# One slot later: scores, outputs and splits in a kernel that interleaves a chunked scan with an MLP

## The chip, the cores and the metric

The kernel runs on one core of a Trainium2 chip. The metric is device time in microseconds: the median of three runs of the kernel before is 1139.93 us (1139.13 to 1140.27). Below, PE is the matrix engine (TensorE), DVE is VectorE, ACT is ScalarE, POOL is GpSimd and SP is SyncE, which here only issues DMAs.

## The reference, cut to what matters

A gated linear recurrence over 768 steps (4 batches, 8 heads of 48), then two gated MLPs (384 to 1536 to 384), the second behind an RMS norm:

```python
for t in range(S):
    state = alpha[:, :, t, :, None] * state + np.einsum('bhd,bhe->bhde', k[:, :, t], v[:, :, t])
    y[:, :, t] = np.einsum('bhd,bhde->bhe', q[:, :, t], state)
...
silu = g * (1.0 / (1.0 + np.exp(-g)))      # g = x @ w_gate
return (silu * val @ w_out)                # val = x @ w_val; second layer: x / rms * rms_g first
```

## The kernel before

The scan is cut into 24 chunks of 128 steps, numbered n = 0 to 23. A chunk is worked in slots T = 0 to 19, and a new chunk starts every 12 slots, so slots T = 12 to 19 of chunk n are the slots T = 0 to 7 of chunk n+1. `chunk(n, T)` (line 468) issues what a slot holds; in a slot the older chunk issues first. All engines run their instructions in the order in which they were issued.

In a chunk, DVE builds products of decays and merges them into q and k at seven levels (T = 0 to 6, `products` and `merge`; the merge at level 64 comes at T = 10), and ACT copies the merged halves (`copy_qk`). PE then makes the scores (`scores`, line 297, T = 8). DVE multiplies the scores of the low levels by masks (`masks`, line 318, T = 9 and 10) and ACT copies those of the two highest (`copies_p`, lines 326 and 329, T = 10). PE transposes k (line 477, T = 11), ACT copies the result to kt (line 529, T = 12), PE makes the outputs in three parts and the update of the state (`own_terms`, `outputs`, `kv`, lines 335 to 380, T = 14 and 16). ACT then copies the chunk's output to xhi, rounded (line 409, T = 17), DVE updates the state (lines 390 and 391, T = 17) and subtracts to get the remainder xlo (line 411, T = 18). Both xhi and xlo feed the MLP. Scores, k transposed and outputs of a chunk all lie in one accumulator tile Y of three banks, one after the other. Between parts of the outputs stands a tiny ACT read of Y ("order", line 485).

The tokens pass the first MLP in seven blocks of 3, 3, 3, 3, 4, 4 and 4 chunks. While PE works on one block, the slots of the next block's chunks are laid between its pieces. A block has 12 hidden steps f of three pieces: piece 0 is the gate product g, piece 1 the value product v, piece 2 the output product o of the hidden step before (nine matmuls each). Slots are issued behind the pieces: one slot behind each piece where the next block has three chunks (block 0, which does its own weight conversion, and blocks 1 and 2), and four slots a hidden step where it has four: one behind g, one behind v and two behind s*v and the o product (blocks 3 to 5). At a block's last piece the last chunk of the next block is at T = 19, so xhi and xlo of that chunk are made just ahead of the next block's first g. DVE multiplies silu(g), made by ACT, with v (line 655, "s"), ACT rounds it to hh (661) and DVE makes its remainder hl (667); o reads hh and hl one hidden step later. A finished block's o banks are copied out by ACT (`evac`, line 606) through two buffers `ev` and stored by SP.

Chunks 0 to 2 ("early", `n < BLOCKS[0][0]`) run ahead of the first block in banks of their own. Input loads stand in SP's queue in slots 15 to 19: q and k of chunk n+2, v of chunk n+1 by levels.

Of the kernel before, what the change touches and what calls it, by code (L numbers as in the profile page):

```python
# [19 lines left out]
B, H, S, D = 4, 8, 768, 48  # L20
# [3 lines left out]
NCH = B * NCB  # L24
# [31 lines left out]
class Kernel:  # L56
# [411 lines left out]
    def chunk(self, n, T):  # L468

        nc = self.nc  # L470
        more = n + B < NCH
        nxt = n + 1 if n + 1 < NCH else None

        if T == 11 and more:
            self.kp = (self.bank(n, "o2") if self.early(n) else self.Y[:, 2]).rearrange("s (p d) -> s p d", p=NP)
            for p in range(NP):
                nc.tensor.transpose(out=self.kp[:, p], in_=self.qk[n % 2][:, 1, p], identity=self.ident)  # L477
        if T == 14:
            self.own_terms(n)
            self.outputs(n, 0)  # L480
            if more:
                self.kv(n)
            self.outputs(n, 1)
        if T == 15 and not self.early(n):
            nc.scalar.activation(out=self.order, in_=self.Y[:, :, 0:1], func=AF.Copy)
        if T == 16:
            self.outputs(n, 2)
        early = self.early(n)
        if T == 6 and early:
            self.scores(n, range(4))  # L490
        if T == (9 if early else 8):
            self.scores(n, range(4 if early else 0, NL))

        if T == (15 if n < B else 17) and n + 2 < NCH:
            self.load_qk(n + 2)
        if T == 17 and nxt:
            self.load_vn(nxt)
        if nxt:
            for l in {17: (0, 1, 2), 18: (3, 4), 19: (5, 6)}.get(T, ()):
                if LEVELS[l] >= CDS[nxt]:  # L500
                    self.load_vl(nxt, l)

        if T == 17:
            self.split_x(n, 0)
            if more:
                self.state(n)
        if T == 18:
            self.split_x(n, 1)
        if T == 0:
            self.start_chunk(n)  # L510
            self.products(n, 1)
        if 1 <= T <= 6:
            self.merge(n, LEVELS[T - 1])
            self.products(n, LEVELS[T])
        if T == (7 if early else 9):
            self.masks(n, range(3))
        if T == 8 and early:
            self.masks(n, [3])
        if T == 10:
            self.masks(n, [4] if early else [3, 4])  # L520
            self.copies_p(n)
            self.merge(n, 64)
        if T == 11 and n >= B:
            for h in range(2):
                o = slice(64 * h, 64 * h + 64)
                nc.scalar.activation(out=self.Sd[o, :, 16 * h:16 * h + 16], in_=self.Sc[n % B][o, :, 32 - 32 * h:D - 32 * h], func=AF.Copy)
        if T == 12 and more:
            kt = self.kt[n] = self.a1.tile([128, NP, 128], F32, tag="kt", name="kt")
            nc.scalar.activation(out=kt, in_=self.kp, func=AF.Copy)
        if T == 1:  # L530
            self.direct = self.direct_ops(n)
        if 1 <= T <= 9:
            k = (1, 2, 2, 1, 2, 2, 2, 2, 9)[T - 1] if CDS[n] > 1 else T > 6
            for _ in range(min(k, len(self.direct))):
                self.direct.pop(0)()
            if T == 9 and nxt:
                for part in range(4):
                    self.load_dir(nxt, part)
# [319 lines left out]
```

## Time and profile before

| | |
|---|---|
| median of three runs | 1139.93 us |
| profiled execution, its own time | 1140.99 us |
| its span | 1139.2 us |
| PE busy | 1073.0 us, 94% |
| DVE busy | 654.4 us, 57% |
| ACT busy | 415.5 us, 36% |

The profiled execution is 1.06 us above the median. Block 0 starts at 69.93 us, block 1 at 172.89, block 2 at 246.64 (these and block 3 with 384 columns), block 4 at 406.36 and block 5 at 508.75 (with 512). A busy PE is full here, so its time is read from the gaps: the view of waits gives, for each engine, who ended its idle time. In a row of the timeline the first number is the start in us from the span's start, the second the time in us from the start of the first to the end of the last instruction of the row, and the bracket is the idle time ahead of it with what ended it. Matmuls overlap, so the next one is issued before the modelled end of the last.

### The profile page before, as it was taken

Reading aid. Unit: us, or ns where it says so; the run is one execution under the profiler, and the core shown is the slowest. Engines: PE = TensorE matmul, PEld = TensorE weight load, DVE = VectorE, ACT = ScalarE, POOL = GpSimd, SP = SyncE. Lnnn points to the kernel's source line nnn. Section 1 sums busy time; section 2 is a strip of 40 time slices with the busy share of each in tenths; the row PEclk is TensorE's granted clock in tenths of the full one; section 3 lists DMA queues with packets and bytes.
Section 4 is the critical chain, followed back from the end, with each engine's and each line's share of the span. In section 5 each row is a group of like instructions: output and inputs, shape, how many; then the busy total and the mean of one; then the engine's idle time right before and its main releaser. Section 6 shows DMA issues by size and latency. Waiting matters only on the chain.

```text
span 1139.2 us, 25598 instructions
## 1 busy us (share of the span) xinstructions
PE 1073.0 (94%) x10944; PEld 890.1 (78%) x10944; DVE 654.4 (57%) x1361; ACT 415.5 (36%) x770; POOL 46.0 (4%) x81
## 2 busy tenths in 40 slices
PE   2668999999999999999999999999999999999997
PEld 2645568999988877777888888888888888888886
DVE  4778867877777776766755877723322323233221
ACT  3456633443343433333334444422231222222212
POOL 2002000000000000000000000000000000000000
PEclk9779999999999999999999999999999999999999
DMA  8656534344354444335415333110000000100000
GB/s 255 178 176 224 158 78 113 96 125 117 103 131 124 124 123 116 109 92 141 118 39 182 123 132 132 42 56 1 28 28 1 28 28 1 56 1 1 28 1 28
DMA packets 56018, 103.64 MB, mean 91 GB/s; under 512 B 7392, under 2 KB 40672, under 8 KB 55904
## 3 DMA queue, kind: packets, MB, share of 16 engines
q1 hardware_dynamic: 50592, 80.37, 24.8%
q0 software_dynamic: 5312, 21.63, 5.7%
q8 instruction: 86, 1.41, 0.5%
q14 instruction: 28, 0.23, 0.1%
HBM read 89.00 MB, written 12.98 MB: 90 GB/s over the span
## 4 chain that ended last, share of the span: by engine, by line
PE 82%; DVE 3%; ACT 2%; DMA 2%; issue 1%; POOL 0%; SPq 0%; ACTq 0%; DVEq 0%
PE v L645 25%; PE g L645 25%; PE o L686 23%; PE Y L340 4%; PE Y L297 3%; DMA x2d<-ev 1%; ACT pt L326 1%; DVE pt L318 1%; PE Y L380 1%; DVE s L655 1%; PE Y L477 1%; ACT ev L606 1%; PE Y L335 1%; PE Y L584 0%; DVE x L167 0%
## 5 line engine op out<-in xcount | busy, mean ns | idle before, releaser
L655 DVE TENSOR_TENSOR s<-s,v 128x512 f32<-128x512 f32 (+1 forms) x156 | 100.7, 646 | 344.5 <-PE v L645 343.3
L645 PE MATMUL v<-xhi,w 128*128 128x512 f32 (+1 forms) x864 | 283.5, 382 | 0.0
L645 PE MATMUL g<-xhi,w 128*128 128x512 f32 (+1 forms) x864 | 282.1, 380 | 0.0
L686 PE MATMUL o<-hh,w 128*128 128x512 f32 (+1 forms) x864 | 208.4, 376 | 0.0
L661 ACT ACTIVATE hh<-s 128x512 fp32r<-128x512 f32 (+1 forms) x144 | 87.2, 606 | 295.3 <-DVE s L655 295.1
L645 PEld LDWEIGHTS v<-xhi,w 128*128 128x128 f32 x864 | 161.2, 188 | 28.1
L645 PEld LDWEIGHTS g<-xhi,w 128*128 128x128 f32 x864 | 161.2, 188 | 27.5
L686 PEld LDWEIGHTS o<-hh,w 128*128 128x128 f32 x864 | 159.7, 188 | 25.7
L652 ACT ACTIVATE s<-g 128x512 f32<-128x512 f32 (+1 forms) x156 | 87.6, 562 | 230.6 <-PE g L645 217.2
L645 PE MATMUL v<-xlo,w 128*128 128x512 f32 (+1 forms) x432 | 162.6, 376 | 0.0
L645 PE MATMUL g<-xlo,w 128*128 128x512 f32 (+1 forms) x432 | 162.6, 376 | 0.0
L686 PE MATMUL o<-hl,w 128*128 128x512 f32 (+1 forms) x432 | 117.9, 379 | 3.8 <-ACT ev L606 3.5
L667 DVE TENSOR_TENSOR hl<-s,hh 128x512 fp32r<-128x512 f32 (+1 forms) x144 | 94.4, 655 | 41.1 <-ACT hh L661 36.8
L686 PEld LDWEIGHTS o<-hl,w 128*128 128x128 f32 x432 | 79.6, 188 | 18.5 <-ACT ev L606 5.4
L645 PEld LDWEIGHTS g<-xlo,w 128*128 128x128 f32 x432 | 81.2, 188 | 12.9
L645 PEld LDWEIGHTS v<-xlo,w 128*128 128x128 f32 x432 | 81.2, 188 | 12.2
L230 DVE TENSOR_TENSOR qk<-qk,bpb 128x512 f32<-128x512 f32 x96 | 65.7, 685 | 9.3 <-ACT kc L253 7.0
L253 ACT ACTIVATE kc<-qk 128x512 f32<-128x512 f32 x72 | 45.3, 629 | 41.2 <-DVE qk L230 40.5
L340 PE MATMUL Y<-pt,vl 64*32 64x64 f32 (+1 forms) x2880 | 48.5, 229 | 4.3 <-issue 3.8
L340 PEld LDWEIGHTS Y<-pt,vl 64*32 64x32 f32 (+1 forms) x2880 | 41.5, 111 | 11.7 <-issue 7.5
L318 DVE TENSOR_TENSOR pt<-Y,mask 128x256 f32<-128x256 f32 x63 | 24.6, 419 | 22.7 <-PE Y L297 22.7
L230 DVE TENSOR_TENSOR qk<-qk,bpa 128x512 f32<-128x512 f32 x48 | 33.0, 687 | 4.7 <-ACT px L253 2.5
(117 smaller groups left out, 1031.1 us busy)
## 6 DMA issues: line engine op xcount, KB each, us to landing
vl<-vl SPq DMA_DIRECT2D x120, 128.0 KB, 3.9
qk<-qka SPq DMA_DIRECT2D x48, 288.0 KB, 4.7
room<-w POOLq DMA_DIRECT2D x36, 384.0 KB, 5.2
dir<-dirx SPq DMA_DIRECT2D x54, 192.0 KB, 3.2
wraw<-w SPq DMA_DIRECT2D x18, 384.0 KB, 3.8
room<-w SPq DMA_DIRECT2D x18, 384.0 KB, 4.1
vn<-vn SPq DMA_DIRECT2D x24, 192.0 KB, 4.7
x2in<-x2d SPq DMA_DIRECT2D x6, 768.0 KB, 4.3
```

The lines of the kernel that those rows point to most:

```text
L230: self.nc.vector.tensor_tensor(out=v, in0=v, in1=sub(t, o, [(1, 2), (2, nb), (0, b)]), op=ALU.mult)
L253: self.nc.scalar.activation(out=sub(t, 0, [(NP * 64, 2), (b, NP * 64 // b), (1, b)]), in_=v, func=AF.Copy)
L297: self.nc.tensor.matmul(out=sc[o:o + w, p] if l < 3 else sc[o:o + w, p // 2, p % 2], lhsT=kc[d, p, gs], rhs=qc[d, p, gs], start=True, stop ...
L318: self.nc.vector.tensor_tensor(out=p, in0=sc, in1=m, op=ALU.mult)
L326: nc.scalar.activation(out=split(self.pt32)[o:o + 32, :, :, g], in_=sc[o:o + 32, :, :, g], func=AF.Copy)
L340: mm = lambda o, a, x: self.nc.tensor.matmul(out=o, lhsT=a, rhs=x, start=False, stop=False, skip_group_check=True)
L645: nc.tensor.matmul(out=ps[:, :N], lhsT=a, rhs=x, start=(q == 0), stop=(q == len(ops) - 1))
L652: nc.scalar.activation(out=s[:, :N], in_=g[:, :N], func=AF.Silu)
L655: nc.vector.tensor_tensor(out=s[:, :N], in0=s[:, :N], in1=v[:, :N], op=ALU.mult)
L661: nc.scalar.activation(out=hh[:, :N], in_=s[:, :N], func=AF.Copy)
L667: nc.vector.tensor_tensor(out=hl[:, :N], in0=s[:, :N], in1=hh[:, :N], op=ALU.subtract)
L686: nc.tensor.matmul(out=O[gj][i][:, :N], lhsT=a[:, 128 * i:128 * i + 128], rhs=x[:, :N], start=(f == 0 and q == 0), stop=(f == NF - 1 and q ...
```

## The change

For chunks 3 to 23 these move: scores T = 8 to 9; masks of levels 1 to 4 from T = 9 to 10 (behind the copies and the merge at 64, which stay at T = 10), of level 8 inside T = 10 to the same place, of level 16 from T = 10 to 11; transposes of k T = 11 to 12; copy to kt 12 to 13; outputs and state product 14 to 15, the order read 15 to 16, third part of the outputs 16 to 17; xhi and state 17 to 18; xlo 18 to 19; loads of q and k for chunk n+2 from 17 to 18 (for chunk 3 from 15 to 18). Nothing is added or taken away.

```diff
-        if T == 11 and more:
+        early = self.early(n)
+        late = 0 if early else 1
+        if T == 11 + late and more:
...
-        if T == 14:
+        if T == 14 + late:
             self.own_terms(n)
             self.outputs(n, 0)
...
-        if T == 15 and not self.early(n):
+        if T == 15 + late and not early:
...
-        if T == 16:
+        if T == 16 + late:
             self.outputs(n, 2)
...
-        if T == (9 if early else 8):
+        if T == 9:
             self.scores(n, range(4 if early else 0, NL))
-        if T == (15 if n < B else 17) and n + 2 < NCH:
+        if T == (15 if early else 18) and n + 2 < NCH:
             self.load_qk(n + 2)
...
-        if T == 17:
+        if T == 17 + late:
             self.split_x(n, 0)
             if more:
                 self.state(n)
-        if T == 18:
+        if T == 18 + late:
             self.split_x(n, 1)
...
-        if T == (7 if early else 9):
+        if T == 7 and early:
             self.masks(n, range(3))
...
         if T == 10:
-            self.masks(n, [4] if early else [3, 4])
             self.copies_p(n)
             self.merge(n, 64)
+            if not early:
+                self.masks(n, range(4))
+        if T == 11 and not early:
+            self.masks(n, [4])
...
-        if T == 12 and more:
+        if T == 12 + late and more:
             kt = self.kt[n] = self.a1.tile([128, NP, 128], F32, tag="kt", name="kt")
```

What this does to the order on the engines is shown at three places, all around the start of block 4 (512 columns; the change shifts line numbers by a few). First PE, the transposes of chunk 16 ("ident,qk_88"), which stand between o of the block before and the second g. Before:

```order
L686 MATMUL o_4297<-hh,w 128x384
L686 MATMUL o_4298<-hh,w 128x384
L477 MATMUL Y<-ident,qk_88 128x128 x4
L645 MATMUL g<-xhi,w 128x512
L645 MATMUL g<-xlo,w 128x512
```

and now they stand between that g and its v:

```order
L651 MATMUL g<-xhi,w 128x512 x2
L651 MATMUL g<-xlo,w 128x512
L651 MATMUL g<-xhi,w 128x512
L479 MATMUL Y<-ident,qk_88 128x128 x4
L651 MATMUL v<-xhi,w 128x512
L651 MATMUL v<-xlo,w 128x512
```

One g pass has come ahead of them; the scores have moved in the same way, from between g and v to between v and o. Second DVE, the masks of chunk 16 ("pt<-Y,mask") beside the multiplication s, the merge at level 64 (L230) and hl, before:

```order
L318 TENSOR_TENSOR pt<-Y,mask 128x256
L421 TENSOR_TENSOR yd<-yd,pr 128x192
L421 TENSOR_TENSOR yd<-yd,dir 128x96
L655 TENSOR_TENSOR s<-s,v 128x512
L318 TENSOR_TENSOR pt<-Y,mask 128x256 x2
L230 TENSOR_TENSOR qk_88<-qk_88,bpb 128x2x4x64
L667 TENSOR_TENSOR hl<-s,hh 128x512
```

and now:

```order
L421 TENSOR_TENSOR yd<-yd,pr 128x192
L421 TENSOR_TENSOR yd<-yd,dir 128x96
L661 TENSOR_TENSOR s<-s,v 128x512
L230 TENSOR_TENSOR qk_88<-qk_88,bpb 128x2x4x64
L318 TENSOR_TENSOR pt<-Y,mask 128x256 x3
L673 TENSOR_TENSOR hl<-s,hh 128x512
```

The first mask has left the place ahead of s, and all three stand behind the merge. Third DVE at the end of block 3, where chunk 15 hands its xlo to block 4, before:

```order
L390 TENSOR_TENSOR S_98<-S_98,bpb 128x192
L391 TENSOR_TENSOR S_98<-S_98,Y 128x192
L230 TENSOR_TENSOR qk_88<-qk_88,bpb 128x2x16x16
L222 TENSOR_TENSOR bpb<-bpb 128x8
L421 TENSOR_TENSOR dir<-dir 128x96
L421 TENSOR_TENSOR pr<-dir 128x96
L655 TENSOR_TENSOR s<-s,v 128x384
L411 TENSOR_TENSOR xlo<-Y,xhi 128x3x128
L230 TENSOR_TENSOR qk_88<-qk_88,bpb 128x2x8x32
```

and now:

```order
L661 TENSOR_TENSOR s<-s,v 128x384
L390 TENSOR_TENSOR S_98<-S_98,bpb 128x192
L391 TENSOR_TENSOR S_98<-S_98,Y 128x192
L230 TENSOR_TENSOR qk_88<-qk_88,bpb 128x2x8x32
L222 TENSOR_TENSOR bpb<-bpb 128x4
L421 TENSOR_TENSOR yd<-dir,w_5259 128x384
L448 TENSOR_REDUCE w_5259<-pr 128x6
L411 TENSOR_TENSOR xlo<-Y,xhi 128x3x128
```

xlo stood right behind s; now the state's two steps and four instructions of the next chunk's slot T = 6 stand between them.

## Rows read from the trace of the kernel before

**Rows 1.** The page, busy time by engine: us, share of the span, instructions.
```profile
PE 1073.0 (94%) x10944; PEld 890.1 (78%) x10944; DVE 654.4 (57%) x1361; ACT 415.5 (36%) x770; POOL 46.0 (4%) x81
```

**Rows 2.** Who waited for whom, PE: us in total, times, longest.
```profile
PE Y L477 <- ACT pt L329: 14.9, 11, 2.4
PE o L686 <- ACT ev L606: 3.5, 4, 1.0
```

**Rows 3.** Timeline, PE, transposes of k: start, us, what, idle before.
```profile
83.45 0.66 PE L477 MATMUL Y<-ident,qk 128*128 128x128 f32 x4 [2.36 <-ACT pt L329]
120.66 0.66 PE L477 MATMUL Y<-ident,qk 128*128 128x128 f32 x4 [1.90 <-ACT pt L329]
350.81 0.66 PE L477 MATMUL Y<-ident,qk 128*128 128x128 f32 x4 [1.41 <-ACT pt L329]
415.52 0.66 PE L477 MATMUL Y<-ident,qk 128*128 128x128 f32 x4 [1.52 <-ACT pt L329]
442.11 0.66 PE L477 MATMUL Y<-ident,qk 128*128 128x128 f32 x4 [1.07 <-ACT pt L329]
```

**Rows 4.** Chain that ended last, 400 to 430: start, us, piece.
```profile
406.52 2.09 PE g L645 x9
408.61 1.54 PE Y L297 x78
427.99 0.81 PE Y L340 x54
```

**Rows 5.** Timeline 439 to 442, PE, DVE and ACT, one chunk's copies.
```profile
439.52 1.52 PE L686 MATMUL o<-hh,w 128*128 128x512 f32 x6
439.11 0.69 DVE L655 TENSOR_TENSOR s<-s,v 128x512 f32<-128x512 f32 x1 [1.31 <-PE v L645]
439.71 0.75 DVE L318 TENSOR_TENSOR pt<-Y,mask 128x256 f32<-128x256 f32 x2
440.56 1.11 ACT L326 ACTIVATE pt<-Y 32x128 f32<-32x128 f32 x4
441.68 0.38 ACT L329 ACTIVATE pt<-Y 128x256 f32<-128x256 f32 x1
```

**Rows 6.** Timeline 504 to 510, a block's end: PE, DVE, ACT.
```profile
508.98 0.39 PE L645 MATMUL g<-xlo,w 128*128 128x512 f32 x1
505.17 0.35 DVE L391 TENSOR_TENSOR S<-S,Y 128x192 f32<-128x192 f32 x1 [1.55 <-ACT xhi L409]
506.91 0.69 DVE L655 TENSOR_TENSOR s<-s,v 128x512 f32<-128x512 f32 x1 [0.24 <-PE v L645]
507.52 0.55 DVE L411 TENSOR_TENSOR xlo<-Y,xhi 128x384 fp32r<-128x384 f32 x1
507.98 0.68 DVE L230 TENSOR_TENSOR qk<-qk,bpb 128x512 f32<-128x512 f32 x1
508.65 0.55 DVE L421 TENSOR_TENSOR yd<-dir,w 128x384 f32<-128x384 f32 x1
509.12 0.45 DVE L448 TENSOR_REDUCE w<-pr 128x6 f32<-128x288 f32 x1
504.65 0.49 ACT L409 ACTIVATE xhi<-Y 128x384 fp32r<-128x384 f32 x1 [0.16 <-PE Y L340]
507.63 0.63 ACT L661 ACTIVATE hh<-s 128x512 fp32r<-128x512 f32 x1 [0.83 <-DVE s L655]
```

**Rows 7.** Timeline, PE, two first matmuls of a block's outputs.
```profile
257.86 0.44 PE L686 MATMUL o<-hl,w 128*128 128x384 f32 x1 [0.63 <-ACT ev L606]
522.37 0.50 PE L686 MATMUL o<-hl,w 128*128 128x512 f32 x1 [1.03 <-ACT ev L606]
```

**Rows 8.** Timeline of the first block, ACT and DVE.
```profile
81.85 1.14 ACT L326 ACTIVATE pt<-Y 32x128 f32<-32x128 f32 x4 [5.14 <-DVE pt L318]
121.79 0.76 DVE L158 TENSOR_SCALAR x<-x 128x1152 f32<-128x1152 f32 x1 [2.18 <-ACT x L151]
123.49 1.36 DVE L167 SCALAR_TENSOR_TENSOR x<-x,room 128x1152 int32<-128x1152 int32 x1 [0.94 <-DMA room<-w]
```

More of the change, by code (lines that the diff above doesn't have):

```diff
@@ L483, in chunk @@
             self.outputs(n, 1)
-        if T == 15 and not self.early(n):
+        if T == 15 + late and not early:
             nc.scalar.activation(out=self.order, in_=self.Y[:, :, 0:1], func=AF.Copy)
-        if T == 16:
+        if T == 16 + late:
             self.outputs(n, 2)
-        early = self.early(n)
         if T == 6 and early:
             self.scores(n, range(4))
-        if T == (9 if early else 8):
+        if T == 9:
             self.scores(n, range(4 if early else 0, NL))
-        if T == (15 if n < B else 17) and n + 2 < NCH:
+        if T == (15 if early else 18) and n + 2 < NCH:
             self.load_qk(n + 2)
@@ L518, in chunk @@
             self.masks(n, [3])
+        if T == 10 and early:
+            self.masks(n, [4])
         if T == 10:
-            self.masks(n, [4] if early else [3, 4])
             self.copies_p(n)
             self.merge(n, 64)
+            if not early:
+                self.masks(n, range(4))
+        if T == 11 and not early:
+            self.masks(n, [4])
         if T == 11 and n >= B:
```

## The prediction

> **What bounds the kernel now.** I read the page's busy times first: PE is busy for 1073.0 us, DVE for 57% of the span [rows 1]. So the time is PE's work plus PE's gaps, and since the change moves instructions and adds none, only the gaps can change. The view of waits, for PE alone, comes next: the largest wait in it is that of the k transposes for the copy at line 329, 14.9 us in 11 waits; the o product waits 3.5 us in 4 for the copying out of the block before [rows 2]. The timeline then says where. Two of the transposes' waits, 2.36 and 1.90 us, lie in block 0; from 328 to 500 us each of the eight chunks 12 to 19 waits: four times 1.41 (chunks 12 to 15), 1.52 once (chunk 16) and three times 1.07 (17 to 19), together 10.37 [rows 3]. One last wait, of 0.23, is left out of the sum. The chunks 6 to 11, at one slot a piece, hardly wait: there a g pass of some 2 us stands between the copies' slot and the transposes'. With four slots a hidden step there is nothing between them.
>
> Why the wait is as long as it is can be followed in one chunk [rows 5]: v ends, s*v starts at 439.11, both masks run from 439.71 to 440.46, only then do the copies start, at 440.56, since they read the same tile behind the masks, and they end at 441.68 + 0.38 = 442.06; the transposes start at 442.11. PE has spent its six last o matmuls by 439.52 + 1.52 = 441.04.
>
> **The change part by part.**
>
> *Transposes behind a g pass: gain 11.6.* Call V the moment PE has issued the last matmul of v in the slot pair with the copies. Now: scores V to V+1.54 [rows 4]; o, nine matmuls of 0.23 (a pass is 2.09), to V+3.6; g to V+5.7; transposes due. The copies need the scores, now on PE behind v instead of ahead of it: they start at about V+1.7, take 1.12 + 0.38 and end at V+3.2, 2.5 us early. The masks wait for the copies now: three of 0.375 [rows 5] end at V+4.4, 1.3 us early. With 384 columns (block 3) the two passes take 0.75 of that, so transposes come due near V+4.9 and the slack on the last mask falls to some 0.5 us. So I take all eight waits as gone: 10.37. The bracket counts from a modelled end: o's six start 0.23 apart, so a seventh would start at 439.52 + 1.38 = 440.90 and 442.11 is 1.21 later, not 1.07. That adds 0.15 to each, 1.2 in all: 11.6. If the cover fails it is as low as 0. Queued behind the masks on DVE while they wait are hl and the next chunk's first product; hl is read by o a whole hidden step later, at about V+8.
>
> *A block's first o: gain 1.4.* At 257.86 and 522.37 o waits 0.63 and 1.03 for a bank to be copied out [rows 7], at the end of a chain from v over s, hh, the copies of P and a store. The scores now stand inside that chain's time, not ahead of it, and their 1.54 fills the wait. The chain starts its copies 0.15 later at the two other block starts, where the transposes' gap is counted already: 1.66 - 0.3, about 1.4; between 0 and 1.7.
>
> *xlo at the ends of blocks 3 and 4: cost 2.9.* PE needs xlo with the second matmul of the next block's first g, 508.98 [rows 6]. Now the third output part (0.81, [rows 4]) stands behind v instead of ahead of it, so s*v starts 0.81 earlier, 506.10, and ends at 506.79; hh (0.63) ends at 507.47, xhi (0.49) at 508.0, the state's sum, which waits for it, at 508.3. Then, ahead of xlo, come the merge and what follows it up to the end of the reduction, 507.98 to 509.12 + 0.37 = 509.49, that is 1.51: 509.8. xlo takes 0.55 and is there at 510.4: PE waits 1.4. At the end of block 3 the same with 384 columns gives 1.5. Both lie two slots behind one piece; where the next block has three chunks xhi comes a piece earlier, and only s*v and xlo are left (0.69 + 0.55 against an o pass of 1.5 or more), so 0 to 0.3 each; chunk 23 has no successor and no state, so 0. Both ends: 0, if the state's sum and the merge run earlier than I place them, to 5.
>
> DVE's own wait for xhi of 1.55 at 505.17, with a ready merge behind it, shows that nothing overtakes there [rows 6]. This is what the Trainium skill states in "PSUM — Partial Sum Buffer", section "Engine vs sequencer instructions": the queues of ScalarE and VectorE are strictly first in, first out. That rule speaks against this change; were xlo free to go as soon as xhi is there, it would be done by 508.6, and the sum would be 2.9 better.
>
> *Block 0: gain 2.0.* Here DVE and ACT convert weights and PE's two gaps of 2.36 and 1.90 are partly slack. But the copies waited 5.14 us for masks at 81.85, and conversion on ACT behind them kept DVE idle at 121.79 for 2.18; a weight load then cost 0.94 [rows 8]. Now the copies wait for scores alone, ACT reaches its conversion earlier, and three masks (1.1) leave the place ahead of it and fill DVE's idle time. The weight load is tied to DVE's conversion before it, so I take about 1 for each of the chunks 3 and 4. Ends: -2 (the q and k load of chunk 5, now three slots later, meets the weight loads) and +4.3 (both gaps).
>
> *Moved at no price.* The kt copy, the order read and the outputs keep their distances from each other and from the transposes. SP issues the q and k load of chunk n+2 behind v and the first levels instead of ahead of them, six slots before use, one and a half hidden steps of over 6 us; if a load came late, the next chunk's first product would wait for it, and s*v behind that product. POOL's queue is unchanged.
>
> Sum: 11.6 + 1.4 - 2.9 + 2.0 = 12.1 off the profiled execution's own 1140.99: 1128.9. The median stands 1.06 lower: 1127.8, so 1128.
>
> **The rivals.**
> - *Block 0 pays in full and xlo is not late.* 11.6 + 1.7 + 4.3 = 17.6: about 1122.5. For: the copies' 5.14 us. Against: the load behind 123.49.
> - *The masks come late.* The last of them, waiting for the copies on a DVE that is late by 0.5 us, stops the transposes in chunks 12 to 15 again and by part in 16 to 19. Half of the 11.6 comes back: 1133.6. For: masks now behind the merge and the copies. Against: DVE is idle before s*v in that place, 1.31 us [rows 5].
> - *The wait only changes hands.* PE then waits as long at g or v for the same chain. No change: 1140. Against: PE has no other wait near it [rows 2].
> - *Slower: every block start waits for xlo.* Place: the first g of each of the six blocks, with all of PE behind it. It decides where six such waits exceed the 15.0 of the other terms, at 2.5 us each; at 3.5 they cost 21 and the time is 1146. For: five to eight DVE instructions now stand between xhi and the end of xlo. Against: my 1.4 at two of them.
>
> By the Trainium skill's page "PSUM — Partial Sum Buffer", section "PSUM bank collisions raise a hardware error", only accesses to one bank must be kept apart, and the transposes write the third bank, the copies read the first two; by that alone there would be no wait and no gain. The rows disagree: the transposes start 0.05 us behind the end of the copy each time [rows 3, 5], so the program's own order of accesses to the tile decides. What that rule would give, no change, is the third rival's time and within its chance.
>
> **How the numbers follow.** Forecast 0.60, with its own range 1124.5 to 1132; the better rival 0.12; late masks 0.13; hands changed 0.07; slower 0.08. No change can be told from a difference under 0.2%, 2.3 us. Faster: 0.60 + 0.12 + 0.13 = 0.85; same 0.07; slower 0.08. The range takes in the better rival and the late masks, with room for block 0's lower end: 1121 to 1137.
>
> **What would show it.** Right: the wait of the transposes for line 329 is gone from PE's waits between 325 and 500 us; g waits for xlo, line 411, for 1 to 2 us at the starts of blocks 4 and 5 and nowhere else; masks wait for the copies, not the copies for masks; the first o of block 5 has no wait. Wrong: transposes that wait for a mask, g waiting for xlo at block 2 or 3, a v that waits for s, or a block 1 that starts no earlier than 172.9.

## The result, and the profile after

| | before | after |
|---|---|---|
| median of four runs each | 1139.62 us | 1123.76 us (1122.81 to 1126.32) |
| profiled execution, its own time | 1140.99 us | 1124.23 us |
| its span | 1139.2 us | 1122.5 us |

The ratio is 0.9864, with a 95% interval of 0.9846 to 0.9882: 15.9 us by the medians, 16.8 by the profiled executions. Forecast were 12.1 less, 1128; the 1123.76 lies inside the forecast's range of 1121 to 1137 and just under the likeliest case's own range of 1124.5 to 1132. What follows looks for the missing 4 us. Two executions of the kernels below took far longer than all others, 2140.55 and 2700.02 us; they stand in the medians of their kernels (chunks 3 to 5 alone, and the load of chunk 5) but not in the ratios and intervals.

First the page's busy times of after, to be laid beside [rows 1]. They are busy time, share of the span and instructions:

```profile
PE 1066.4 (95%) x10944; PEld 887.4 (79%) x10944; DVE 655.1 (58%) x1361; ACT 415.8 (37%) x770; POOL 45.6 (4%) x81
```

The instruction counts are the same. PE's busy time has fallen from 1073.0 by 6.6 us although its work is the same. By stretches of the two traces, 2.2 of the 6.6 lie ahead of block 0, where PE is busy for only half of the time, 3.3 in block 0 and 1.1 in blocks 3 and 4. In block 0 the granted clock was higher, as shown below. So the forecast's opening step, that only gaps can change, was too narrow for this pair of executions. That the change itself raises the clock is not shown: the four executions of the changed kernel have mean granted clocks of 0.984 to 0.992, and the profiled one has the highest. Next the waits of PE in after (who waited for whom, us in total, times, longest), which answer to [rows 2]:

```profile
PE g L651 <- DVE xlo L411: 2.5, 3, 1.2
PE Y L479 <- DVE pt L318: 2.2, 1, 2.2
PE o L692 <- ACT ev L612: 1.5, 3, 0.5
PE v L651 <- DVE s L661: 1.4, 1, 1.4
PE Y L335 <- DMA yn<-ydd: 1.2, 1, 1.2
```

The line that led before, transposes (now L479) for the copy at L329, 14.9 us in 11, is not there any more. What stands there are new waits: g for xlo, one transpose for a mask, one v for s, and the transposes of yn (the chunk's direct terms) for their load. On DVE and ACT the same view shows that the order has turned:

```profile
DVE pt L318 <- ACT pt L329: 15.8, 18, 1.4
DVE S L391 <- ACT xhi L409: 19.8, 15, 3.1
```

Masks wait for copies, 18 times; before, the copies waited for masks, 35.6 us in 15 waits. Of these, 14.8 us belong to the three early chunks, which keep their order and wait as long after, and 19.0 to the three chunks of block 0. The timeline of one chunk in block 4 answers to [rows 5], with PE first:

```profile
423.25 0.39 PE L651 MATMUL v<-xhi,w 128*128 128x512 f32 x1
423.57 1.14 PE L297 MATMUL Y<-kc 64*64 64x64 f32 x47
425.92 1.53 PE L692 MATMUL o<-hh,w 128*128 128x512 f32 x6
425.26 0.69 DVE L230 TENSOR_TENSOR qk<-qk,bpb 128x512 f32<-128x512 f32 x1 [0.83 <-PE Y L297]
426.80 1.09 DVE L318 TENSOR_TENSOR pt<-Y,mask 128x256 f32<-128x256 f32 x3 [0.84 <-ACT pt L329]
425.26 1.11 ACT L326 ACTIVATE pt<-Y 32x128 f32<-32x128 f32 x4 [0.17 <-PE Y L297]
426.38 0.38 ACT L329 ACTIVATE pt<-Y 128x256 f32<-128x256 f32 x1
429.34 0.60 PE L479 MATMUL Y<-ident,qk 128*128 128x128 f32 x4
```

Take V = 423.48, 0.23 behind the start of v's last matmul. The copies start at V+1.8 and end at V+3.3, the masks end at V+4.4, and the transposes come at V+5.9 with no bracket. The forecast had 1.7, 3.2, 4.4 and 5.7.

Then the two places where the forecast saw a price, the starts of blocks 4 and 5, to be laid beside [rows 6]. In the timeline of after at the start of block 4:

```profile
392.02 0.55 DVE L661 TENSOR_TENSOR s<-s,v 128x384 f32<-128x384 f32 x1 [1.43 <-PE v L651]
393.04 0.47 ACT L409 ACTIVATE xhi<-Y 128x384 fp32r<-128x384 f32 x1
393.54 0.35 DVE L391 TENSOR_TENSOR S<-S,Y 128x192 f32<-128x192 f32 x1 [0.70 <-ACT xhi L409]
393.81 0.69 DVE L230 TENSOR_TENSOR qk<-qk,bpb 128x512 f32<-128x512 f32 x1
394.49 0.55 DVE L421 TENSOR_TENSOR yd<-dir,w 128x384 f32<-128x384 f32 x1
394.96 0.45 DVE L448 TENSOR_REDUCE w<-pr 128x6 f32<-128x288 f32 x1
395.32 0.55 DVE L411 TENSOR_TENSOR xlo<-Y,xhi 128x384 fp32r<-128x384 f32 x1
395.92 0.50 PE L651 MATMUL g<-xlo,w 128*128 128x512 f32 x1 [1.20 <-DVE xlo L411]
```

The state's sum waits for xhi, the merge, one product and the reduction stand behind it, and xlo ends at 395.87; the g that wants it starts 0.05 us later. The same at two other block starts, and the new wait for a load at the end of block 3:

```profile
166.90 0.44 PE L651 MATMUL g<-xlo,w 128*128 128x384 f32 x1 [0.43 <-DVE xlo L411]
386.30 0.52 PE L335 MATMUL Y<-ident,yn 128*128 128x128 f32 x3 [1.20 <-DMA yn<-ydd]
492.71 0.50 PE L651 MATMUL g<-xlo,w 128*128 128x512 f32 x1 [0.91 <-DVE xlo L411]
```

To see where the time went, subtract the starts of the first g of successive blocks in each trace (one profiled execution each):

| block | before, us | after, us | difference | what the waits account for |
|---|---|---|---|---|
| 0 | 102.51 | 96.30 | -6.2 | forecast 2.0 less, at best 4.3 |
| 1, 2 | 74.20, 73.82 | 74.08, 73.67 | -0.1, -0.2 | nothing moved there |
| 3 | 85.90 | 80.75 | -5.15 | transposes 4 x 1.56, first o 0.4, less 1.20 for yn |
| 4 | 102.39 | 97.08 | -5.3 | transposes 5.33, first o 1.0, less xlo 1.20 |
| 5 | 94.00 | 93.84 | -0.2 | first o 1.03, less xlo 0.91 |

Block 1's first g starts at 172.44 us before; the 172.89 given above is 0.45 too late. The rest of the program is 0.8 us longer, 0.47 of it a first o of block 6 that now waits, and the start 0.4 shorter. So the blocks with 11.6 us of transposes' waits gave what they were said to give, and the surplus of this pair lies in block 0.

Block 0's own gaps are told best by PE's rows of the timeline with a bracket. Before, from 100 to 120 us (the next one is [rows 3]'s 1.90, at 120.66):

```profile
100.25 2.20 PE L645 MATMUL v<-x,x 128*128 128x384 f32 x6 [0.52 <-DVE s L655]
106.73 3.80 PE L645 MATMUL g<-x,x 128*128 128x384 f32 x6 [2.34 <-ACT s L652]
```

After, in the whole of block 0 behind its first pass:

```profile
83.88 0.63 PE L479 MATMUL Y<-ident,qk 128*128 128x128 f32 x4 [2.21 <-DVE pt L318]
89.78 2.20 PE L651 MATMUL v<-x,x 128*128 128x384 f32 x6 [1.40 <-DVE s L661]
99.58 0.88 PE L340 MATMUL Y<-pt,vl 64*32 64x64 f32 x64 [1.29 <-ACT order L487]
112.01 0.34 PE L297 MATMUL Y<-qk 64*64 64x64 f32 x5 [1.38 <-issue]
```

A gap of 2.34 that the prediction didn't have is gone, and with it a slow pass: 3.80 us for the same six matmuls that take 2.10 in after. The view by stretches gives the length, then the busy time of PE, and, as the third number from the end, the clock that PE was granted, as a share of full speed. The whole of block 0 and five us of it, before:

```profile
69.93:172.44 102.51, 93.28 (x1312) 57.99 (x1312) 83.00 (x140) 53.35 (x83) 12.06 (x21) 0.95 0.49 149
105.00:110.00 5.00, 3.27 (x5) 1.83 (x6) 4.97 (x9) 5.00 (x6) 1.91 (x3) 0.66 0.19 46
```

After:

```profile
69.53:165.83 96.30, 90.01 (x1311) 56.86 (x1312) 82.47 (x138) 53.55 (x83) 11.66 (x21) 0.98 0.51 158
105.00:110.00 5.00, 5.00 (x125) 3.30 (x127) 4.97 (x7) 2.83 (x3) 1.29 (x3) 1.00 0.77 263
```

Behind its idle 2.34 us PE ran that pass partly at the lower of its two levels, 1.2 instead of 2.4 GHz: 0.66 on the mean of the five us. So the one place took 2.34 + 1.70 = 4.0 us in this trace. Over the whole of block 0, PE's gaps are 9.23 us before and 6.28 after, 2.95 less; the other 3.27 of the 6.2 are busy time. Of these, 1.70 are that slow pass, and most of the rest lies at the block's start, where PE comes out of a wait of some 4 us: the granted clock from 70 to 75 us is 0.50 before and 0.68 after, from 75 to 80 it is 0.92 and 1.00.

The slow pass does not belong to that gap, as two more traces with block 0 as before show. In the kernel with only the transposes of chunks 6 to 23 late (below), the same g waits as long and then runs at full speed; a slow pass stands behind another gap, the transposes' at 120.42, which is 3.49 long there:

```profile
106.49 2.20 PE L646 MATMUL g<-x,x 128*128 128x384 f32 x6 [2.36 <-ACT s L653]
121.33 4.05 PE L646 MATMUL v<-x,x 128*128 128x384 f32 x6
```

With chunks 6 to 23 alone changed, g waits 1.98 and takes 2.20 too, and the slow passes (3.16 and 2.77) stand behind the transposes' 2.35 at 81.08. In these three traces block 0 is 101.3 to 104.1 us long, with gaps of 9.2 to 10.3; in the six with all slots late and the masks behind the copies it is 96.3 to 98.5 long, with gaps of 4.4 to 7.1. By the means that is 5.2 us less, 3.5 in gaps and 1.7 in busy time, and the pair compared here lies a us over it.

On the other two engines the timeline of before tells where the wait came from:

```profile
103.02 0.48 ACT L409 ACTIVATE xhi<-Y 128x384 fp32r<-128x384 f32 x1
103.53 0.36 DVE L387 COPY S<-Y 128x192 f32<-128x192 f32 x1 [1.28 <-ACT xhi L409]
103.80 0.68 DVE L230 TENSOR_TENSOR qk<-qk,bpb 128x512 f32<-128x512 f32 x1
104.52 0.63 ACT L253 ACTIVATE qk<-qk 128x512 f32<-128x512 f32 x1 [1.02 <-DVE qk L230]
105.05 1.25 ACT L151 ACTIVATE x<-room 128x1152 f32<-128x1152 f32 x1
106.19 0.48 ACT L652 ACTIVATE s<-g 128x384 f32<-128x384 f32 x1
```

DVE's copy into the state of chunk 3 waits for xhi, the next chunk's merge stands behind it, ACT's copy of that merge waits for the merge, a piece of weight conversion stands behind that, and silu, which g waits for, stands last. In after xhi and the state come a slot later, silu of that pass starts at 102.81, and PE does not wait.

### The profile page after: what moved, and what is told of

Read it like the earlier page. It is cut to its first block, busy times and chain, and to the rows that moved or that the text cites. A ratio compares the mean times of both kernels' runs of the same rounds, so it can differ in the third digit from the quotient of the medians.

```text
span 1122.5 us, 25564 instructions
## 1 busy us (share of the span) xinstructions
PE 1066.4 (95%) x10944; PEld 887.4 (79%) x10944; DVE 655.1 (58%) x1361; ACT 415.8 (37%) x770; POOL 45.6 (4%) x81
## 4 chain that ended last, share of the span: by engine, by line
PE 85%; DVE 2%; DMA 2%; ACT 1%; issue 1%; SPq 0%; ACTq 0%; DVEq 0%; POOLq 0%
PE g L651 25%; PE o L692 25%; PE v L651 25%; PE Y L340 4%; PE Y L297 3%; DMA x2d<-ev 1%; PE Y L380 1%; PE Y L335 1%; PE Y L479 1%; PE Y L590 0%; DMA ydd<-yd 0%; PE Y L571 0%; DVE qk L230 0%; DMA room<-w 0%; ACT ev L612 0%
## 5 line engine op out<-in xcount | busy, mean ns | idle before, releaser
L651 PE MATMUL v<-xhi,w 128*128 128x512 f32 (+1 forms) x864 | 280.2, 378 | 0.0
L692 PE MATMUL o<-hl,w 128*128 128x512 f32 (+1 forms) x432 | 122.0, 389 | 1.7 <-ACT ev L612 1.5
L692 PEld LDWEIGHTS o<-hl,w 128*128 128x128 f32 x432 | 76.9, 188 | 17.3 <-ACT ev L612 2.5
L230 DVE TENSOR_TENSOR qk<-qk,bpb 128x512 f32<-128x512 f32 x96 | 65.9, 687 | 25.8 <-PE Y L297 15.3
L230 DVE TENSOR_TENSOR qk<-qk,bpa 128x512 f32<-128x512 f32 x48 | 32.9, 686 | 4.5 <-ACT px L253 2.8
```

Source lines behind the costliest of these rows:

```text
L230: self.nc.vector.tensor_tensor(out=v, in0=v, in1=sub(t, o, [(1, 2), (2, nb), (0, b)]), op=ALU.mult)
L651: nc.tensor.matmul(out=ps[:, :N], lhsT=a, rhs=x, start=(q == 0), stop=(q == len(ops) - 1))
L692: nc.tensor.matmul(out=O[gj][i][:, :N], lhsT=a[:, 128 * i:128 * i + 128], rhs=x[:, :N], start=(f == 0 and q == 0), stop=(f == NF - 1 and q ...
```

## The experiments

There are two theories on the surplus. **A**: in block 0 the copies' wait for masks held up ACT's weight conversion [rows 8], and the order of masks and copies gave most of the gain. **B**: the slots gave it, as pieces now stand between scores, copies, transposes and splits. First the change was cut in two by chunks, then one term at a time was tried.

**The change for chunks 3 to 5 alone, and for 6 to 23 alone.**

```diff
-        early = self.early(n)
-        late = 0 if early else 1
+        (self.chunk_new if n < 6 else self.chunk_old)(n, T)
```

and the other way round in the second kernel. Expected of the first:

> The change for chunks 3 to 5 alone (those laid into block 0); chunks 6 to 23 as in the kernel before. Theory A (block 0 gave some 6 us: in the trace of after block 1 starts about 6 us earlier, and PE's clock no longer falls at 106 us): 1133.4, and block 1 starts near 166. Theory B (block 0 gave the 2.0 of the prediction and the rest came from the later blocks): 1137.6.

and of the second:

> The change for chunks 6 to 23 alone; chunks 3 to 5 as in the kernel before. Theory A (the later blocks gave the 11.6 + 1.4 - 2.9 of the prediction, about 10): 1129.6, with g waiting 1.20 and 0.91 for xlo at the starts of blocks 4 and 5. Theory B (the later blocks gave nearly all): 1125.7.

Measured: 1134.93 against 1139.82 (ratio 0.9961, 0.9948 to 0.9973) for chunks 3 to 5, and 1127.61 (0.9899, 0.9880 to 0.9918) for 6 to 23. The product of the ratios is 0.9860, the whole change's 0.9864: the two parts add up. Chunks 3 to 5 alone give 4.9 us by the medians and 4.4 by the ratio, more than twice the 2.0 of the forecast; the interval, 3.1 to 5.9, leaves out the 2.0 but not the forecast's upper end of 4.3. In the trace block 0 is 98.44 long and the waits of the transposes for L329 in the later chunks are back, 10.6 us in 9. Chunks 6 to 23 give 12.2 by the medians, where the forecast's terms without block 0 make 10.1, and between the two theories; the interval, 9.3 to 13.7, holds the 10.1. In its trace g waits 1.20 and 0.92 us for xlo at the starts of blocks 4 and 5, as said. So block 0 paid clearly more than forecast; that the rest did is not shown.

**xlo ahead of the state.** The changed kernel, with xlo issued right behind xhi in its new slot:

```diff
         if T == 17 + late:
             self.split_x(n, 0)
+            if late:
+                self.split_x(n, 1)
             if more:
                 self.state(n)
-        if T == 18 + late:
+        if T == 18 and early:
             self.split_x(n, 1)
```

> The changed kernel with xlo issued right behind xhi, ahead of the state's two steps and of the next chunk's slot. If DVE's queue order is what makes PE wait for xlo at a block's start: the waits of 0.43, 1.20 and 0.91 go, some 2.5 us, 1121.3. Rival (DVE stands for xhi in either order and the time goes to the state and the merge behind it, which are late for something else): 1123.8, no change.

Measured: 1120.32 (1118.80 to 1123.57), ratio to before 0.9835 (0.9810 to 0.9860). No g waits for xlo. The same place as above, start of block 4, in this trace:

```profile
392.05 0.47 ACT L409 ACTIVATE xhi<-Y 128x384 fp32r<-128x384 f32 x1
392.56 0.56 DVE L411 TENSOR_TENSOR xlo<-Y,xhi 128x384 fp32r<-128x384 f32 x1 [0.97 <-ACT xhi L409]
393.34 0.39 PE L653 MATMUL g<-xhi,w 128*128 128x512 f32 x1
393.57 0.40 PE L653 MATMUL g<-xlo,w 128*128 128x512 f32 x1
```

xlo is done at 393.12, before the block's first g, and the second matmul follows the first 0.23 us later. So the wait was the queue ahead of xlo and nothing else. The change costs this 2.5 us by its waits; the medians differ by 3.4.

**xlo ahead of the state in three chunks only**, 5, 15 and 19, the ones that PE waited for:

```diff
-            if late:
+            if n in (5, 15, 19):
                 self.split_x(n, 1)
...
-        if T == 18 and early:
+        if T == 18 + late and n not in (5, 15, 19):
             self.split_x(n, 1)
```

> The changed kernel, with xlo ahead of the state only for chunks 5, 15 and 19, whose xlo PE waited for (0.43, 1.20 and 0.91 us); in all other chunks xlo stands a slot later, as in the changed kernel. Theory (only a block's last xlo is on PE's path): as fast as with xlo early in all chunks, 1120.3 to 1121.5, no g waits for xlo. Rival (the early xlo helped in other places as well): 1122.5 or more.

Measured: 1121.66 (1119.76 to 1123.84), ratio 0.9849 (0.9833 to 0.9864), and no g waits for xlo. It is 0.16 us over the theory's band and under the rival's: the last xlo of a block is what counts, and what the early xlo gives elsewhere is not more than this measurement can tell. The intervals of both these kernels touch that of the changed kernel, so that they are faster than it rests on the vanished waits as well as on the medians.

**Only the transposes and the kt copy a slot later**, for chunks 6 to 23, all else as before:

```diff
-        if T == 11 and more:
+        late = 1 if n >= 6 else 0
+        if T == 11 + late and more:
...
-        if T == 12 and more:
+        if T == 12 + late and more:
```

> The kernel before with one thing moved: for chunks 6 to 23 the transposes of k and the kt copy one slot later, all else where it was. If the one g pass between copies and transposes is what pays: PE's wait for line 329 goes in chunks 12 to 19, 11.6 us, 1128.0, and nothing is paid for xlo. Rival (the scores' move is needed too, since the kt copy now stands one slot ahead of the outputs): part of the wait comes back at the outputs, 1132 or more.

Measured: 1130.39 (0.9923, 0.9901 to 0.9945), 9.4 us less than before. The view of PE's waits of this kernel:

```profile
PE Y L478 <- ACT pt L329: 5.8, 2, 3.5
PE o L687 <- ACT ev L607: 5.4, 4, 2.5
```

The two waits for L329 that are left lie in block 0; from chunk 6 on none is left. This edit alone moves the transposes behind a g pass, and the masks stay ahead of the copies: the distance is enough. It falls 2.4 us short of the theory's 1128. In the trace the first o of the blocks waits 5.4 us in place of 3.5 [rows 2]; but 2.54 of it stand at block 3 alone, where before has 0.85, and the execution traced, 1133.74, is the slowest of the four. What does not move with this edit is the first o's wait for the copying out: it is 2.9 to 3.7 us in the five traces whose chunks 6 to 23 are as before, and 0.8 to 1.5 in the seven that have all their steps late. So the forecast's second term needs more than the transposes' move. That it is the scores' move which pays for it fits, but the scores were not moved alone.

**Block 0, the order alone and the slots alone.** The kernel before, with the masks of chunks 3 to 5 behind the copies:

```diff
+        behind = 3 <= n < 6
...
-            self.masks(n, [4] if early else [3, 4])
+            if not behind:
+                self.masks(n, [4] if early else [3, 4])
             self.copies_p(n)
             self.merge(n, 64)
+            if behind:
+                self.masks(n, range(4))
+        if T == 11 and behind:
+            self.masks(n, [4])
```

> The kernel before, with one edit for chunks 3 to 5 alone: the copies of the highest scores and the merge at 64 are issued ahead of the masks, the mask of level 16 a slot behind them. Scores, transposes, outputs and splits stay in their old slots. Theory A (in block 0 the copies' wait for masks held up ACT's weight conversion, 5.14 us at 81.85 and 8.05 at 119.11, and that is most of what block 0 gained): the time falls by about 4 of the 4.9 us that chunks 3 to 5 gave together, to 1136; the two waits of the copies become waits for scores, and block 0 is some 98 us long. Theory B (the slots matter: a piece of PE between copies and transposes): transposes still come right behind the copies, now wait for masks behind them, and the time is 1139 or more, block 0 some 102.

and the changed kernel, with them ahead of the copies again:

```diff
+        if T == 10 and ahead:
+            self.masks(n, range(5))
         if T == 10:
             self.copies_p(n)
             self.merge(n, 64)
-            if not early:
+            if not early and not ahead:
                 self.masks(n, range(4))
```

> The changed kernel, with the masks of chunks 3 to 5 issued ahead of their copies again, all in the slot of the copies; all slots stay late. Theory A (the order of masks and copies): block 0 loses most of its gain, 1123.8 + 4 = 1128. Theory B (the slots): 1124 to 1125, and block 0 stays near 97 us.

Measured: the order alone 1136.98 against 1139.80 (0.9979, 0.9968 to 0.9991), the slots without the order 1126.23 (0.9884, 0.9868 to 0.9899). The one gains 2.8 us, the other loses 2.3 to 2.5 against the changed kernel (1123.94 in the same series, below, and 1123.76): they agree, and both lie between the theories. The order is about half of block 0's gain; block 0 is 99.7 and 99.4 us long in their traces, between 102.5 and 96.3. In the kernel with the order alone the long gap stands as before, the slow pass behind it too, in PE's rows of the timeline:

```profile
104.60 3.83 PE L651 MATMUL g<-x,x 128*128 128x384 f32 x6 [2.34 <-ACT s L658]
```

**Block 0, the splits alone.** The kernel before, with xhi, state and xlo of chunks 3 to 5 a slot later:

```diff
-        if T == 17:
+        later = 1 if 3 <= n < 6 else 0
+        if T == 17 + later:
             self.split_x(n, 0)
...
-        if T == 18:
+        if T == 18 + later:
             self.split_x(n, 1)
```

> The kernel before, with one edit for chunks 3 to 5 alone: xhi, the state and xlo come a slot later; scores, masks, transposes and outputs stay. Theory (in the old slot DVE's copy into the state waits for xhi, 1.28 us at 103.53, the merge behind it and ACT's copy of that merge are late with it, silu stands behind them, and PE's g waits 2.34 us at 106.73 and then runs its pass in 3.80 us instead of 2.10): that wait and the slow pass go, 2 to 4 us, to 1136 to 1138; the copies' wait for masks near 82 and 119 stays. Rival (the gain of the slots comes from scores and transposes): 1139.8, within 1 us, and g still waits near 107.

Measured: 1138.29 against 1139.06 (0.9992, 0.9983 to 1.0001). Most of g's gap is gone, and no slow pass follows it, as the theory has it, in PE's rows of the timeline:

```profile
103.07 2.20 PE L646 MATMUL g<-x,x 128*128 128x384 f32 x6 [0.49 <-ACT s L653]
106.35 0.76 PE L297 MATMUL Y<-px 64*32 64x32 f32 x64 [1.08 <-DVE xlo L411]
111.95 2.63 PE L646 MATMUL v<-x,x 128*128 128x384 f32 x5 [2.77 <-issue]
114.37 3.08 PE L687 MATMUL o<-s,x 128*128 128x384 f32 x6
```

But two new gaps come behind it, 1.08 for xlo ahead of the scores of chunk 4 and 2.77 at a v, and behind the second stand slow passes: five matmuls of v in 2.63 us, where order and splits together (below) take 1.88, and six of o in 3.08 instead of 2.10. The granted clock is 0.79 from 110 to 115 us and 0.86 from 115 to 120. The time keeps 0.8 us of the 4.0, and its interval holds no change. The local reading was right, the size was not.

**Order and splits together**, both diffs in the kernel before:

> The kernel before, with both single edits for chunks 3 to 5: masks behind the copies, and xhi, state and xlo a slot later. Scores, transposes and outputs stay in their old slots. Theory (these two delays of ACT and DVE are what block 0 gained): the whole 4.4 to 4.9 us of chunks 3 to 5, to 1135, block 0 some 97 to 98 us. Rival (the slots of scores and transposes carry a share of their own): the two single edits' 2.8 and 0.8 us add up to 3.6 at most, 1136.2 or more.

Measured: 1138.86 against 1140.36 (0.9984, 0.9973 to 0.9996). Neither the 4.4 to 4.9 of the theory nor more than the order alone: the rival holds, so the slots of scores, transposes and outputs carry a share, though none of the three was tried alone. Its trace (of its shortest run, 1135.43) has the same wait, 1.09, for xlo ahead of the scores, and 2.26 at the v. The whole change has neither; there the scores have moved away from xlo as well.

**The load of q and k of chunk 5** back to its old place in the changed kernel:

```diff
-        if T == (15 if early else 18) and n + 2 < NCH:
+        if T == (15 if n < B else 18) and n + 2 < NCH:
```

> The changed kernel, with the load of q and k of chunk 5 issued three slots earlier again, in block 0 as in the kernel before. Theory (that load's place costs nothing): 1123.8, within 1 us. Rival (the prediction's lower end for block 0: in its new place it meets the weight loads and costs up to 2 us): 1122.

Measured: 1123.94, or 1123.45 without the execution of 2700.02 (0.9855, 0.9840 to 0.9871): the changed kernel's time. No price of the load's place shows, though the interval, 1121.6 to 1125.1 us, still holds the rival's 1122.

**The mask that the transposes of chunk 3 wait for.** In the kernel with xlo ahead of the state, the mask of level 16 goes right behind the others in chunks 3 to 5:

```diff
-                self.masks(n, range(4))
-        if T == 11 and not early:
+                self.masks(n, range(5 if n < 6 else 4))
+        if T == 11 and n >= 6:
             self.masks(n, [4])
```

> The kernel with xlo ahead of the state, and for chunks 3 to 5 also the mask of level 16 right behind the other masks instead of one slot later, behind a stretch of weight conversion. In block 0 the transposes of chunk 3 wait 2.2 us at 83.9 for that mask. Theory (that wait is on PE's path in block 0): 1120.3 - 2 = 1118.3. Rival (PE then waits as long at the next gate product or conversion): 1120.3, within 0.7.

Measured: 1122.21 (0.9852, 0.9831 to 0.9872), not faster than 1120.32. The transposes' 2.21 is gone, and in the timeline the v behind it waits instead:

```profile
89.31 2.91 PE L653 MATMUL v<-x,x 128*128 128x384 f32 x6 [3.81 <-DVE s L663]
```

3.81 in place of 2.21 + 1.40. DVE is busy for 90.0 of the 110 us from 60 to 170 in the changed kernel. That it sets the pace there fits, as the gap of PE that was filled opened again at the next thing that DVE makes, but no run made DVE's work there less.

## Why the prediction was right, and where it was off

*Transposes behind a g pass, 11.6.* Right in place, mechanism and size. The eight waits are gone; blocks 3 and 4 are 10.45 us shorter, and with the 1.20 that xlo and the 1.20 that the yn load cost there, 12.9, of which 1.4 belongs to the first o of the two blocks, the next term. That leaves 11.5. The masks did not come late: they end 1.4 us ahead of the transposes in the chunk above, where 1.3 was said, and 0.5 ahead in block 3, as said. The edit of transposes alone confirmed the mechanism, with 9.4 us and none of these waits left.

*A block's first o, 1.4.* Right in kind, small in size: 3.5 us of waits became 1.5, 2.0 less. The one at 522.37 [rows 7] is gone, as said; that at 257.86 did not go but shrank from 0.63 to 0.53. The sum had counted nothing at blocks 3 and 4, whose waits went from 0.85 to 0.47 and from 1.01 to nothing; block 6 has a new one of 0.47.

*xlo at the ends of blocks 3 and 4, 2.9.* Right in place and chain, somewhat too large: 1.20 and 0.91 by the view of waits, or 1.36 and 1.07 counted as the forecast counted, from where the matmul was due, 0.23 behind the first; 1.5 and 1.4 stood there. "And nowhere else" was wrong: 0.43 at the start of block 1, where 0 to 0.3 was said. By the waits 2.5 in all; xlo moved ahead of the state gave it back. The rule of the Trainium skill in "PSUM — Partial Sum Buffer", section "Engine vs sequencer instructions", that VectorE's queue is strictly first in, first out, agrees with it: nothing overtook the 1.5 us between the state's sum and xlo until the program itself did.

*Block 0, 2.0: the step that was mis-sized.* It measured 4.4 to 4.9 us alone and 6.2 in the profiled pair, of which 3.3 is busy time at a lower clock that changes from execution to execution. The prediction took the copies' wait and ACT's conversion behind it, about 1 for each of two chunks; that part, the order of masks and copies, measured 2.3 to 2.8. It had laid two rows together that lie 40 us apart: ahead of DVE's idle 2.18 at 121.79 stand not the copies that waited 5.14 at 81.85 but those of chunk 4 at 119.11, which waited 8.05. What it left out is the wait of g for silu at 106.73; this row was not read, since the two gaps of the transposes were taken for block 0's whole stock of 9.23. The splits' new slot removes that wait, but alone it gives 0.8, and with the order not more than the order alone. So about half of the gain is the order; the other half comes with the slots of scores, transposes, outputs and splits together, and how it splits among them is open.

*Moved at no price.* The load of q and k was put at nothing, and no price of it shows. Not seen: the yn load of chunk 15, which made PE wait 1.20. POOL's queue is unchanged, but its store of yd waits to land before the load is issued, and that took 5.14 us instead of 3.47, as the timelines show, after:

```profile
383.10 0.75 POOL L465 DMA_DIRECT2D yn<-ydd  x1 [5.14 <-DMA ydd<-yd]
```

and before:

```profile
393.82 0.75 POOL L465 DMA_DIRECT2D yn<-ydd  x1 [3.47 <-DMA ydd<-yd]
```

Why the store took longer wasn't tried.

By parts the misses are: block 0 +4.2 (profiled pair), first o +0.6, xlo +0.4, the yn load -1.2, the rest of the tail -0.3, the earlier start +0.4; with the 12.1 of the sum that makes 16.2 of the 16.8, and what is left is within the spread of single executions (block 0 alone varies by 2.2 in the six traces above).

Of the signs, those named for a right forecast came, but for the extra wait at block 1 and a 0.91 just under its 1 to 2 us. Two of the signs named for a wrong one came as well, both in block 0: the transposes of chunk 3 wait 2.21 for a mask (83.88), and the v behind them 1.40 for s (89.78). They did not undo the forecast, since it counted on no more than 2.0 us from block 0 and the waits of the blocks that carry the sum were gone.

Of the rivals, "block 0 pays in full" came nearest with 1122.5, half for its reason: block 0 did pay, past its 4.3, but xlo was late. The late masks, the wait that changes hands and the slower case, xlo at every block start, did not come.

## What to carry to other kernels

When a wait is removed in a stage that waits in many places, list all of the engine's gaps there, not only those that the change names: the two that were counted here are 4.3 of 9.2 us. Do not price a gap by a slow pass that one trace shows behind it: another execution had that pass elsewhere. An edit that moves steps by a slot should be tried part by part in such a stage, and together, since the medians of the parts need not add (0.8 and 2.8 alone, 1.5 together, 4.9 with all). And where a consumer on the critical path waits for the last instruction of a pair, put that pair together ahead of work with slack: with xlo ahead of the state this kernel's median is 1120.32 us, the lowest seen here, though its interval touches that of the changed kernel.

## What the runs showed of the hardware

After 2.34 us without work PE's next six matmuls took 3.80 us instead of 2.10, at a mean granted clock of 0.66 over the five us around them; in the kernel with the order alone the same pair was 2.34 and 3.83. The same gap need not be followed by such a pass: with only the transposes of chunks 6 to 23 late it was 2.36 and 2.20. The same holds for the transposes' gap of chunk 3 in the changed order: behind the 2.21 at 83.88 in after the next passes took 2.10 each, and in the kernel with the load of chunk 5 back in its place, behind 2.21 at 85.00, the next o pass took 3.50. A gap of 1.93 us was followed by slow passes (3.23 and 2.80, with chunks 3 to 5 alone, at a granted clock of 0.86 and 0.80 over the ten us from 110), and one of 2.26 was not (order and splits together). What tells the two apart these runs do not show.

DVE overtook nothing. With xhi done at 393.51 us in after, xlo stood 1.8 us behind work that was issued ahead of it; issued ahead of that work, it started 0.04 us behind xhi, at 392.56.
